# Attention and token mixing on one core: the 64-wide matmuls as four 64x64 tiles, whole-array transposes, and a written order of steps

## The chip, the core and the metric

The kernel runs on one core of one Trainium2 chip. TensorE (PE in the profile) multiplies and transposes, VectorE (DVE) and ScalarE (ACT) read its results out of PSUM, GpSimd (POOL) casts the inputs, and SyncE (SP) issues most transfers. The metric is the device time of one execution in microseconds (us); the number given for a kernel is the median over its runs.

PSUM has eight banks of 512 float32 columns on 128 partitions. A matmul names the part of the 128x128 array it uses by the partitions of its operands: 64 input partitions use half of the rows, 64 output partitions half of the columns. The profile writes this as 128\*128, 128\*64 (rows\*columns), 64\*128; a 64\*64 matmul uses one quarter.

## What is computed

```python
# q, k, v: (8 batches, 12 heads, 448 tokens, 64); float32 in and out
scores = q @ k.transpose(0, 1, 3, 2) / sqrt(64) - log(448)
attn   = sigmoid(scores)
x      = (attn @ v)  # heads side by side: (8, 448, 768)
wq, wk = x @ w_q, x @ w_k                        # (8, 448, 64) each
W_tok  = einsum('bsd,btd->bst', wq, wk) / sqrt(64)
out    = maximum(einsum('bst,btd->bsd', W_tok, x), 0) @ w_out   # (8, 448, 768)
```

The kernel works in bfloat16 with float32 sums. It never forms `W_tok`: it takes `wk` transposed times `x` first (`tmp`, 64 x 768 for a batch) and then `wq` times `tmp` (`mix`).

## The kernel before

The work is cut into 24 pairs. Pair n = (u, j) takes batches 2u, 2u+1 and heads 2j, 2j+1: four units of 448 x 448 scores. Six pairs (j = 0 to 5) make a stage u, four stages the kernel. The scheduler is off: each engine runs its instructions in the order in which the code issues them, and waits where a tile or a PSUM buffer is not ready.

For a pair, SP loads q, k (one transfer of 448 KB each) and v (four transfers, since the two batches are laid out differently); POOL casts them to bfloat16. Loads run three pairs ahead for q and k (two for v), casts two ahead (one for v).

- `tr_q`, `tr_k` (L133, L148) transpose the next pair, 64 columns at a time: 14 matmuls for q, 16 for k, of which two read a tile of zeros. Two run side by side in the two column halves. DVE copies the result out.
- `scores(n, g)` (L182), g = 0 to 5: keys 128 at a time with 64 contraction rows, two matmuls side by side in the two row halves (64\*128), one per batch. The 448 keys of a head are three blocks of 128 and 64 left over; `scores_last` (L173) takes what is left over of both heads and batches with 128 rows, half of them zeros (128\*64). Each step fills one double bank and ACT takes it through one sigmoid of 896 columns (`sigmoid`, L168). Two double banks alternate.
- `values(n, h)` (L195): 128 keys of contraction, two batches side by side in the column halves, eight matmuls per head, and one DVE copy per head.
- `tr_x` (L212) transposes the result for `tmp`, again 64 at a time with zeros.
- Once a stage: `mlp_wqk` (24 matmuls), `mlp_wkn` (16 transposes), `mlp_tmp` (16), `mlp_mix` (12, each with one relu: batch 0 on DVE, batch 1 on ACT), and 14 output chunks `mlp_out` of six full matmuls (128\*128, 384 columns), a DVE copy each and two output transfers per two chunks.

The order on PE within a pair is the body of the main loop (from L359): `tr_q(n+1)`, `scores_last`, `tr_k(n+1)`, `tr_x(n-2)`, two scores, output chunks, two scores, both `values(n-1)`, two scores, and then `mlp_wqk` of the stage before (j = 0), all of `mlp_mix` (j = 1), or more chunks (j = 2 to 5). Chunks of stage u are spread over the pairs of stage u+1: four in j = 2 and 3, two in j = 4, 5, 0, 1 (four throughout in the last stage). Everything that is not a score shares four single banks. After pair 23 the tail runs the last values, the whole token mixing of stage 3 and its 14 chunks.

Of the kernel before, what the change touches and what calls it, by code (L numbers as in the profile page):

```python
# [16 lines left out]
def kernel(  # L17
# [16 lines left out]

    nc = tc.nc
    B, H, S, HD = q.shape
    D = H * HD
# [19 lines left out]
    p_w32 = pool("w32", 3)  # L57
# [6 lines left out]
    p_o = pool("o", 4)  # L64
    ps_s = pool("ps_s", 2, space=bass.MemoryType.PSUM)
    ps_f = pool("ps_f", 4, space=bass.MemoryType.PSUM)

    NV = 3
    v32 = [singles.tile([P, 2, 2, 4, HD], F32, name=f"v32{n}") for n in range(NV)]
# [7 lines left out]
    zero16 = singles.tile([P, NP], BF16)  # L77
# [7 lines left out]
    ld = {}  # L85

    def load1(n, nm, eng):
# [10 lines left out]
    def load_v(n, eng):  # L98

        u, j = pairs[n]  # L100
        t = v32[n % NV]
        for b2 in range(2):
            base = v[2 * u + b2, 2 * j]
            for par in range(2):
                s0, s1, i0 = ((0, 4, 0), (0, 3, 4), (1, 4, 0), (0, 4, 3))[2 * b2 + par]
                eng.dma_start(
                    out=t[HALF[par], b2, :, s0:s1, :].rearrange("p h s d -> p h (s d)"),
                    in_=bass.AP(
                        base.tensor, base.offset + i0 * HD,
                        [[NI * HD, NP], [S * HD, 2], [1, (s1 - s0) * HD]],  # L110
                    ),
                )

    def cast1(n, nm, eng):
        t16 = p_c16.tile([P, 2, NI, HD], BF16, tag=nm + "16", name=nm + "16")
        eng.tensor_copy(  # L116
            out=t16.rearrange("p b i d -> p b (i d)"), in_=ld.pop((nm, n))
        )
        ld[nm + "16", n] = t16

    v16s = {}

    def cast_v(n):
        t = p_v16.tile([P, 2, 2, 4, HD], BF16, tag="v16", name="v16")
        nc.gpsimd.tensor_copy(  # L125
            out=t.rearrange("p b h s d -> p (b h s d)"),
            in_=v32[n % NV].rearrange("p b h s d -> p (b h s d)"),
        )
        v16s[n] = t


    qts, kts = {}, {}

    def tr_q(n):
        ps = ps_f.tile([P, NI, 2, NP], BF16, tag="f", name="ptq")
        t16 = ld.pop(("q16", n))
        for i in range(NI):
            for b2 in range(2):
                nc.tensor.transpose(  # L139
                    ps[HALF[b2], i].rearrange("p h n -> p (h n)"), t16[:, b2, i, :], ident16  # L140
                )
        t = p_qk.tile([P, 2, S], BF16, tag="qt", name="qt")
        nc.vector.tensor_copy(  # L143
            out=t.rearrange("p h (i n) -> p h i n", i=NI), in_=ps.rearrange("p i h n -> p h i n")
        )
        qts[n] = t

    def tr_k(n):  # L148
        ps = ps_f.tile([P, 8, 2, NP], BF16, tag="f", name="ptk")
        t16 = ld.pop(("k16", n))  # L150
        order = (0, 4, 1, 5, 2, 6, 3, 3)
        for pos in range(8):
            for b2 in range(2):
                src = zero16 if (pos, b2) in ((6, 1), (7, 0)) else t16[:, b2, order[pos], :]
                nc.tensor.transpose(  # L155
                    ps[HALF[b2], pos].rearrange("p h n -> p (h n)"), src, ident16
                )
        t = p_qk.tile([P, 2, 4 * P], BF16, tag="kt", name="kt")
        nc.vector.tensor_copy(  # L159
            out=t.rearrange("p h (s n) -> p h s n", s=8), in_=ps.rearrange("p s h n -> p h s n")  # L160
        )
        kts[n] = t
# [4 lines left out]
    def sigmoid(n, key, sc):  # L167
        at = p_at.tile([P, 2, S], BF16, tag="at", name="at")  # L168
        nc.scalar.activation(at, sc[:, :, 0:S], ACTF.Sigmoid, bias=bias_t, scale=attn_scale)  # L169
        ats[n, key] = at  # L170

    def scores_last(n):

        sc = ps_s.tile([P, 2, 512], F32, tag="s", name="sc")
        for h in range(2):
            for b2 in range(2):
                nc.tensor.matmul(  # L177
                    sc[HALF[b2], h, 0:S], kts[n][:, h, 3 * P + 64 * b2 : 3 * P + 64 * b2 + 64],
                    qts[n][:, h, :], start=True, stop=True,
                )  # L180
        sigmoid(n, 6, sc)

    def scores(n, g):
        h, m = divmod(g, 3)
        sc = ps_s.tile([P, 2, 512], F32, tag="s", name="sc")
        for b2 in range(2):
            nc.tensor.matmul(  # L187
                sc[:, b2, 0:S], kts[n][HALF[b2], h, m * P : (m + 1) * P], qts[n][HALF[b2], h, :],
                start=True, stop=True,
            )  # L190
        sigmoid(n, g, sc)


    xts = {}

    def values(n, h):
        u, j = pairs[n]
        ps = ps_f.tile([P, S], F32, tag="f", name="pv")
        for m in range(4):
            for b2 in range(2):  # L200
                slot = m + b2 if m < 3 else 3 * (1 - b2)
                rhs = ats[n, 3 * h + m][:, b2, :] if m < 3 else ats[n, 6][:, h, :]
                nc.tensor.matmul(  # L203
                    ps[HALF[b2]], v16s[n][:, b2, h, slot, :], rhs, start=(m == 0), stop=(m == 3)
                )
        t = p_x.tile([P, S], BF16, tag=f"xt{2 * j + h}", name="xt")
        nc.vector.tensor_copy(out=t, in_=ps)  # L207
        xts[u, 2 * j + h] = t
# [4 lines left out]
    def tr_x(n):  # L213
# [3 lines left out]
        ps = ps_f.tile([P, 4, 2, 2, HD], BF16, tag="f", name="px")  # L217
        for h in range(2):
            for m in range(4):
                for par in range(2):  # L220
                    i = 2 * m + par
                    src = xts[u, 2 * j + h][:, i * NP : (i + 1) * NP] if i < NI else zero16
                    nc.tensor.transpose(ps[HALF[par], m, :, h, :], src, ident16)  # L223
        nc.vector.tensor_copy(  # L224
            out=xns[u][:, :, :, 2 * HD * j : 2 * HD * (j + 1)].rearrange("p m b x -> p (m b) x"),
            in_=ps.rearrange("p m b h d -> p (m b) (h d)"),
        )


    wqk, wkn, tmps, mxs = {}, {}, {}, {}  # L230

    def mlp_wqk(u):
        ps = [ps_f.tile([P, S], F32, tag="f", name="pw") for _ in range(2)]
        for h in range(H):
            for b2 in range(2):
                nc.tensor.matmul(  # L236
                    ps[b2], wqk16[HALF[b2], h, :], xts[u, h][HALF[b2]],
                    start=(h == 0), stop=(h == H - 1),
                )
        wqk[u] = [p_one.tile([P, S], BF16, tag=f"wqk{b2}", name="wqk") for b2 in range(2)]  # L240
        for b2 in range(2):
            nc.vector.tensor_copy(out=wqk[u][b2], in_=ps[b2])

    def mlp_wkn(u):
        ps = ps_f.tile([P, 4, 2, P], BF16, tag="f", name="pk")
        for b2 in range(2):
            for m in range(4):
                for par in range(2):
                    i = 2 * m + par
                    src = wqk[u][b2][:, i * NP : (i + 1) * NP] if i < NI else zero16  # L250
                    nc.tensor.transpose(ps[HALF[par], m, b2, :], src, ident16)  # L251
# [3 lines left out]
        )  # L255

    def mlp_tmp(u):
        tmps[u] = p_one.tile([P, D], BF16, tag="tmp", name="tmp")
        for nb in range(2):
            ps = ps_f.tile([P, NB], F32, tag="f", name="pt")  # L260
            for m in range(4):
                for b2 in range(2):
                    nc.tensor.matmul(  # L263
                        ps[HALF[b2]], wkn[u][:, m, 64 * b2 : 64 * b2 + 64],
                        xns[u][:, m, b2, nb * NB : (nb + 1) * NB],
                        start=(m == 0), stop=(m == 3),
                    )
            nc.vector.tensor_copy(out=tmps[u][:, nb * NB : (nb + 1) * NB], in_=ps)  # L268

    def mlp_mix(u, c):  # L270
        if c == 0:
            mxs[u] = [p_one.tile([P, 2, S], BF16, tag=f"mx{n}", name="mx") for n in range(NC)]
        ps = [ps_f.tile([P, S], F32, tag="f", name="pm") for _ in range(2)]
        for b2 in range(2):
            nc.tensor.matmul(  # L275
                ps[b2], tmps[u][HALF[b2], c * P : (c + 1) * P], wqk[u][b2][HALF[b2]],
                start=True, stop=True,
            )
        nc.vector.tensor_scalar(mxs[u][c][:, 0, :], ps[0], moe_scale, 0.0, ALU.mult, ALU.max)  # L279
# [173 lines left out]
```

## Time and profile before

| | us |
|---|---|
| median of 3 runs (250.43 to 252.59) | 250.77 |
| the profiled execution | 250.65 |
| its span, first to last instruction | 248.5 |
| a stage in mid-kernel, from values to values (112.19 to 167.07) | 54.9 |
| from the last scores (216.86) to the end | 31.6 |

The profiled execution spends 2.15 us outside its span. A row of the grouped view reads: line, engine, operation, result from sources, shape, count, then busy time, the mean duration of one in ns, and the idle time before it. Durations on PE overlap: a matmul of 448 columns lasts about 0.36 us from issue to its modelled end, while in a dense stream a pair of them side by side passes in about half of that. So the PE durations that count here are taken from the chain of waits, where each piece ends where the next begins.

### The profile page before, as it was taken

The numbers are of one execution on the slowest core, as the hardware profiler recorded it, in microseconds if no ns is written. First come the engines' busy times: TensorE is split into PE (matmuls) and PEld (weight loads), VectorE is DVE, ScalarE is ACT, GpSimd is POOL, SyncE is SP. The second block draws the span as 40 slices with busy tenths as digits, with TensorE's granted clock in tenths as the row PEclk, the third lists the DMA queues.
The fourth block names the chain that finished last, engine by engine and source line by source line (L and its number), as shares of the span: only waits on it lengthen the run. The fifth ranks groups of instructions, "written<-read, shape, count | busy, mean of one in ns | idle before, by whom it ended". The sixth has DMA issues, their size and how long they took to land.

```text
span 248.5 us, 6124 instructions
## 1 busy us (share of the span) xinstructions
PE 215.9 (87%) x2480; PEld 116.7 (47%) x2480; DVE 132.2 (53%) x230; ACT 171.7 (69%) x194; POOL 75.5 (30%) x84
## 2 busy tenths in 40 slices
PE   0878777779779999999979999999979999998992
PEld 0534334445435644545544554455444554453660
DVE  2423444454575555564685654655684564458551
ACT  2499889986677768986688678895698678724000
POOL 1655466566302131441633041343631010000000
PEclk9979999999979999999999999999999999999997
DMA  6999999999900498789872489789962543220376
GB/s 239 303 286 268 249 330 318 308 296 262 247 2 21 115 275 231 187 231 286 224 216 65 114 240 263 211 234 259 234 170 66 130 105 95 67 63 3 79 201 163
DMA packets 35387, 47.58 MB, mean 191 GB/s; under 512 B 6432, under 2 KB 31008, under 8 KB 35360
## 3 DMA queue, kind: packets, MB, share of 16 engines
q1 hardware_dynamic: 35088, 46.74, 70.2%
q8 instruction: 19, 0.31, 0.6%
q10 hardware_dynamic: 272, 0.46, 0.5%
q14 instruction: 8, 0.07, 0.1%
HBM read 36.18 MB, written 11.01 MB: 190 GB/s over the span
## 4 chain that ended last, share of the span: by engine, by line
PE 72%; ACT 17%; issue 5%; DVE 2%; DMA 2%; ACTq 0%
PE po L289 19%; PE pv L203 16%; ACT at L169 15%; PE sc L187 12%; PE ptk L155 5%; PE ptq L139 5%; PE sc L177 5%; PE px L223 4%; PE pw L236 4%; ACT mx L280 2%; PE pt L263 2%; DMA q<-in_q_dram 2%; PE pm L275 1%; DVE tmp L268 1%; PE pk L251 1%
## 5 line engine op out<-in xcount | busy, mean ns | idle before, releaser
L169 ACT ACTIVATE at<-sc,bias_t 128x896 bf16<-128x896 f32 x168 | 158.8, 1006 | 49.3 <-PE sc L177 23.7
L289 PE MATMUL po<-wout,mx 128*128 128x384 bf16 x336 | 59.6, 327 | 0.1
L187 PE MATMUL sc<-qt,kt 64*128 64x448 bf16 x288 | 47.2, 358 | 14.4 <-ACT at L169 14.0
L294 DVE COPY o<-po 128x384 f32<-128x384 f32 x56 | 31.2, 558 | 37.7 <-PE po L289 36.6
L207 DVE CAST xt<-pv 128x448 bf16<-128x448 f32 x48 | 30.0, 625 | 39.6 <-PE pv L203 36.4
L289 PEld LDWEIGHTS <-mx 128*128 128x128 bf16 x336 | 30.6, 98 | 25.2 <-issue 7.2
L203 PE MATMUL pv<-at,v 128*64 128x448 bf16 x384 | 40.9, 356 | 0.0
L116 POOL CAST q<-q 128x896 bf16<-128x896 f32 x23 | 21.5, 933 | 59.0 <-DMA q<-in_q_dram 29.9
L125 POOL CAST v<-v 128x1024 bf16<-128x1024 f32 x24 | 25.0, 1040 | 38.4 <-PE pv L203 21.0
L187 PEld LDWEIGHTS <-kt 64*128 64x128 bf16 x288 | 12.3, 93 | 43.3 <-issue 40.8
L116 POOL CAST k<-k 128x896 bf16<-128x896 f32 x24 | 22.6, 940 | 24.5 <-DMA k<-in_k_dram 16.9
L203 PEld LDWEIGHTS <-v 128*64 128x64 bf16 x384 | 19.7, 109 | 17.0 <-issue 6.1
L159 DVE COPY kt<-ptk 128x1024 bf16<-128x1024 bf16 x24 | 16.6, 690 | 9.7 <-PE ptk L155 9.7
L139 PE MATMUL ptq<-ident,q 128*64 128x128 bf16 x336 | 15.5, 238 | 6.0 <-DVE q L116 6.0
L143 DVE COPY qt<-ptq 128x896 bf16<-128x896 bf16 x24 | 15.0, 624 | 8.6 <-PE ptq L139 8.5
L139 PEld LDWEIGHTS <-q 128*64 128x64 bf16 x336 | 11.3, 119 | 14.2 <-issue 6.5
L280 ACT ACTIVATE mx<-pm 128x448 bf16<-128x448 f32 x24 | 11.7, 550 | 8.1 <-PE pm L275 8.0
L155 PEld LDWEIGHTS <-k 128*64 128x64 bf16 x336 | 15.1, 120 | 4.2 <-issue 0.8
L224 DVE COPY xn<-px 128x1024 bf16<-128x1024 bf16 x24 | 16.4, 681 | 0.4 <-PE px L223 0.4
L177 PE MATMUL sc<-qt,kt 128*64 128x448 bf16 x96 | 14.5, 382 | 2.2 <-ACT at L169 2.2
L155 PE MATMUL ptk<-ident,k 128*64 128x128 bf16 x336 | 16.4, 233 | 0.0
L279 DVE TENSOR_SCALAR mx<-pm 128x448 bf16<-128x448 f32 x24 | 13.8, 619 | 2.6 <-PE pm L275 2.4
(36 smaller groups left out, 125.5 us busy)
## 6 DMA issues: line engine op xcount, KB each, us to landing
q<-in_q_dram SPq DMA_DIRECT2D x24, 448.0 KB, 5.9
out_dram<-o SPq DMA_DIRECT2D x56, 192.0 KB, 2.7
k<-in_k_dram SPq DMA_DIRECT2D x23, 448.0 KB, 7.0
v<-in_v_dram SPq DMA_DIRECT2D x48, 128.0 KB, 6.0
v<-in_v_dram SPq DMA_DIRECT2D x48, 96.0 KB, 5.6
w<-in_moe_w_out_dram SPq DMA_DIRECT2D x6, 384.0 KB, 6.2
k<-in_k_dram ACTq DMA_DIRECT2D x1, 448.0 KB, 4.9
wqk<-in_moe_w_q_dram SPq DMA_DIRECT2D x2, 192.0 KB, 6.4
```

The source lines that it names most:

```text
L116: eng.tensor_copy(out=t16.rearrange("p b i d -> p b (i d)"), in_=ld.pop((nm, n)))
L125: nc.gpsimd.tensor_copy(out=t.rearrange("p b h s d -> p (b h s d)"), in_=v32[n % NV].rearrange("p b h s d -> p (b h s d)"),)
L139: nc.tensor.transpose(ps[HALF[b2], i].rearrange("p h n -> p (h n)"), t16[:, b2, i, :], ident16)
L155: nc.tensor.transpose(ps[HALF[b2], pos].rearrange("p h n -> p (h n)"), src, ident16)
L169: nc.scalar.activation(at, sc[:, :, 0:S], ACTF.Sigmoid, bias=bias_t, scale=attn_scale)
L177: nc.tensor.matmul(sc[HALF[b2], h, 0:S], kts[n][:, h, 3 * P + 64 * b2 : 3 * P + 64 * b2 + 64], qts[n][:, h, :], start=True, stop=True,)
L187: nc.tensor.matmul(sc[:, b2, 0:S], kts[n][HALF[b2], h, m * P : (m + 1) * P], qts[n][HALF[b2], h, :], start=True, stop=True,)
L203: nc.tensor.matmul(ps[HALF[b2]], v16s[n][:, b2, h, slot, :], rhs, start=(m == 0), stop=(m == 3))
L207: nc.vector.tensor_copy(out=t, in_=ps)
L280: nc.scalar.activation(mxs[u][c][:, 1, :], ps[1], ACTF.Relu, bias=0.0, scale=moe_scale)
L289: nc.tensor.matmul(ps, mxs[u][c].rearrange("p b s -> p (b s)")[:, m * P : (m + 1) * P], wout16[:, c, nb * NB : (nb + 1) * NB], start=(c == ...
L294: nc.vector.tensor_copy(out=ot[0][:, nb * NB : (nb + 1) * NB], in_=ps)
```

## The change

- Scores go by 64 keys: seven steps a pair, each four matmuls of 64 rows and 64 columns, one in each quarter of the array (batch picks the rows, head the columns). `scores_last` and its zeros go. The sigmoids stay 168 of 896 columns.
- Values go by 64 keys too: seven steps of four matmuls, gathered in one double bank; one DVE copy of 896 columns in place of two of 448.
- `mlp_wqk` (12 steps) and `mlp_mix` (6 steps) are cut from two 64\*128 matmuls to four 64\*64 a step.
- All transposes take 128 x 128: seven for q, seven for k, eight for x, eight for `mlp_wkn`. The zero tile goes; `xt` and `wqk` get 64 zero columns at the end, written once by POOL (seven memsets).
- v is loaded and cast as q and k are: one transfer in place of four.
- PSUM: three double banks in turn (scores, values, wqk, mix) and two single ones.
- The order on PE is a string for each pair, with one letter a step: S scores, P values of pair n-1, q and k transposes for n+1, x `tr_x(n-2)`, W wqk, N wkn, U tmp, M mix, O a chunk. Chunks now start in j = 2 (four, then three a pair), 13 in a stage; three are left for the tail.
- At the start 44 small matmuls on the identity run before the first transposes, k of pair 0 is cast half by POOL and half by ACT, and the first copies are split by head. In the tail ACT shares the copies and issues half of the output transfers. `o` has three buffers (four before), `w32` two (three), `mx` two (one).

Core of the diff:

```diff
-    ps_s = pool("ps_s", 2, space=bass.MemoryType.PSUM)
-    ps_f = pool("ps_f", 4, space=bass.MemoryType.PSUM)
+    free2 = ["a", "b", "c"]
+    free1 = ["d", "e"]
...
-            in_=dict(q=q, k=k)[nm][2 * u : 2 * u + 2, 2 * j : 2 * j + 2].rearrange(
+            in_=SRC[nm][2 * u : 2 * u + 2, 2 * j : 2 * j + 2].rearrange(
...
+        for i in range(NI):
+            nc.tensor.transpose(
+                ps[:, i].rearrange("p h n -> p (h n)"),
+                t16[:, i].rearrange("p b d -> p (b d)"), ident16,
+            )
...
+    def scores(n, i):
+        fb, sc = bank2("sc")
+        for b2 in range(2):
+            for h in range(2):
+                nc.tensor.matmul(
+                    sc[HALF[h], b2, 0:S], qk["k", n][HALF[b2], h, i, :],
+                    qk["q", n][HALF[b2], h].rearrange("p i n -> p (i n)"), start=True, stop=True,
+                )
+        at = p_at.tile([P, 2, S], BF16, tag="at", name="at")
+        nc.scalar.activation(at, sc[:, :, 0:S], ACTF.Sigmoid, bias=bias_t, scale=attn_scale)
+        free2.append(fb)
...
+        for h in range(2):
+            for b2 in range(2):
+                nc.tensor.matmul(
+                    ps[HALF[b2], h, 0:S], ld["v16", n][HALF[h], i, b2, :],
+                    ats[n, i][HALF[h], b2, :], start=(i == 0), stop=(i == NI - 1),
+                )
+        if i == NI - 1:
+            nc.vector.tensor_copy(out=xts[j][:, :, 0:S], in_=ps[:, :, 0:S])
+            free2.append(fb)
...
+        ("SqkSPPPSxSSPPPPSS",) * 6,
...
+            "S qk S PPP S x S O S PPPP S O S O",
...
-    mlp_wqk(NU - 1)
+    run(N, "xPPPPPPP WWWWWWWWWW OO WW")
```

The first string is that of stage 0, the second that of j = 3, 4 and 5 of the later stages. The string of j = 0 holds seven S, seven P, qk, x and twelve W; that of j = 1 seven S, N, qk, x, seven P, two U and four M; that of j = 2 adds the last two M and four O.

ACT's queue around the mixing of stage 0 (`at` a sigmoid, `mx` a relu of 448 columns). Before:

```order
L90 DMA k_106<-in_k_dram 128x2x448
L328 ACT_TABLE_LOAD
L328 ACTIVATE warm<-bias_t 128x1
L169 ACTIVATE at<-sc,bias_t 128x896 x56
L280 ACTIVATE mx<-pm 128x448 x6
L169 ACTIVATE at<-sc,bias_t 128x896 x42
```

And now:

```order
L354 CAST k_180<-k_112 128x7x64
L158 ACTIVATE at<-sc,bias_t 128x896 x55
L257 ACTIVATE mx<-pm 128x448 x2
L158 ACTIVATE at<-sc,bias_t 128x896
L257 ACTIVATE mx<-pm 128x448 x2
```

The six relus stood in one block after the last sigmoid of j = 1; they now come in twos between its last sigmoids and the first of j = 2.

DVE's queue from the mixing of stage 0 through j = 2 of stage 1 (`xn` copies of `tr_x`, `xt` of values, `o` of chunks). Before:

```order
L279 TENSOR_SCALAR mx<-pm 128x448 x6
L143 COPY qt<-ptq 128x896
L159 COPY kt<-ptk 128x1024
L224 COPY xn<-px 128x8x128
L294 COPY o<-po 128x384 x2
L207 CAST xt<-pv 128x448 x2
```

And now:

```order
L259 TENSOR_SCALAR mx<-pm 128x448 x2
L195 COPY xn<-px 128x4x128 x2
L299 COPY o<-po 128x384
L177 CAST xt_102<-pv 128x2x448
L299 COPY o<-po 128x384 x3
L137 COPY qt<-ptq 128x896
L137 COPY kt<-ptk 128x896
```

The chunk copies are spread singly over the pair instead of in two twos; values take one copy a pair, and `tr_x` two.

More of the change, by code (lines that the diff above doesn't have):

```diff
@@ L148, in tr_k @@
[L148 to L162, printed above, removed]
@@ L216, in tr_x @@
             xns[u] = p_x.tile([P, 4, 2, D], BF16, tag="xn", name="xn")
-        ps = ps_f.tile([P, 4, 2, 2, HD], BF16, tag="f", name="px")
+        fb, ps = bank([P, 4, 2, 2, HD], BF16, "px")
         for h in range(2):
             for m in range(4):
[L220 to L235, printed above, removed]
+                nc.tensor.transpose(
+                    ps[:, m, h].rearrange("p b d -> p (b d)"), xts[j][:, h, m * P : (m + 1) * P],
+                    ident16,
+                )
@@ L255, in mlp_wkn @@
         )
[L257 to L268, printed above, removed]
+        free1.append(fb)
@@ new lines, in mlp_tmp @@
+    def mlp_tmp(u, nb):
+        if nb == 0:
+            tmps[u] = p_one.tile([P, D], BF16, tag="tmp", name="tmp")
+        fb, ps = bank([P, NB], F32, "pt")
+        for m in range(4):
+            for b2 in range(2):
+                nc.tensor.matmul(
+                    ps[HALF[b2]], wkn[u][:, m, 64 * b2 : 64 * b2 + 64],
+                    xns[u][:, m, b2, nb * NB : (nb + 1) * NB],
+                    start=(m == 0), stop=(m == 3),
+                )
+        dst = tmps[u][:, nb * NB : (nb + 1) * NB]
+        if nb and u == NU - 1:
+            nc.scalar.copy(out=dst, in_=ps)
+        else:
+            nc.vector.tensor_copy(out=dst, in_=ps)
+        free1.append(fb)
@@ L282, with out_chunk @@
+        for b2 in range(2):
+            relu(mxs[u][c][:, b2, :], ps[:, b2, 0:S], b2)
+        free2.append(fb)
+    chunks = []
     ot = {}
-    def mlp_out(u, m, nb):
+    def out_chunk(tail=False):
+        u, m, nb = chunks.pop(0)
         if nb == 0:
             ot[0] = p_o.tile([P, D], F32, tag="o", name="o")
-        ps = ps_f.tile([P, NB], F32, tag="f", name="po")
+        o = ot[0]
+        fb, ps = bank([P, NB], F32, "po")
         for c in range(NC):
@@ L344 @@
-    tr_q(0)
-    tr_k(0)
+    k0 = ld.pop(("k", 0)).rearrange("p b (i d) -> p b i d", i=NI)
+    k016 = p_c16.tile([P, NI, 2, HD], BF16, tag="k16", name="k16")
+    nc.gpsimd.tensor_copy(out=k016[:, :, 0, :], in_=k0[:, 0])
+    nc.scalar.copy(out=k016[:, :, 1, :], in_=k0[:, 1])
+    ld["k16", 0] = k016
+    eq = tr(0, "q", split=True)
+    eq(slice(0, 1))
+    ek = tr(0, "k", split=True)
+    for hs in (slice(0, 1), slice(1, 2)):
+        ek(hs)
+        if hs.start == 0:
+            eq(slice(1, 2))
```

308 lines of the change are left out of this document (155 added, 153 removed), and 5 rows, old and new, of the table BASE.

## The prediction

> **What bounds the kernel now.** I read the busy shares first, then the chain of waits, then the windows between pair and pair, and last the timeline of ACT.
>
> ```profile
> PE 215.9 (87%) x2480; PEld 116.7 (47%) x2480; DVE 132.2 (53%) x230; ACT 171.7 (69%) x194; POOL 75.5 (30%) x84
> PE 72%; ACT 17%; issue 5%; DVE 2%; DMA 2%; ACTq 0%
> ```
>
> PE is the bound, but the second line shows ACT carrying a sixth of the chain: the two take turns. The windows (length, then busy us by engine) tell where. The first is stage 0 from pair 2 on, the next six the pairs j = 0 to 5 of one stage, the last the tail.
>
> ```profile
> 22.20:51.10 28.90, 22.05 (x316) 12.06 (x316) 12.76 (x21) 26.09 (x29) 17.39 (x19) 1.00 1.09 296
> 107.75:116.58 8.83, 8.54 (x110) 4.55 (x112) 4.24 (x7) 7.34 (x8) 2.10 (x3) 1.00 0.86 227
> 116.58:128.83 12.25, 10.57 (x130) 5.49 (x132) 9.16 (x17) 8.74 (x12) 5.68 (x6) 1.00 0.91 253
> 128.83:138.09 9.26, 9.26 (x105) 5.12 (x106) 5.33 (x9) 7.31 (x9) 2.85 (x3) 1.00 0.20 51
> 138.09:147.34 9.25, 9.25 (x105) 5.07 (x106) 5.35 (x9) 6.72 (x7) 1.20 (x2) 1.00 0.81 225
> 147.34:154.99 7.65, 7.37 (x93) 3.89 (x94) 4.24 (x7) 5.88 (x7) 2.34 (x3) 1.00 0.81 219
> 154.99:162.63 7.64, 7.36 (x92) 3.89 (x94) 4.24 (x7) 6.61 (x8) 3.06 (x4) 1.00 0.81 229
> 216.86:248.50 31.64, 25.48 (x212) 13.99 (x210) 17.24 (x31) 5.14 (x9) 0.00 (x0) 0.96 0.39 100
> ```
>
> In j = 2 and 3 PE never rests (9.26 of 9.26). In j = 1, the longest pair by 3 us, neither engine is full: PE 10.57, ACT 8.74 of 12.25. In stage 0 (7.2 us a pair) ACT is busy 90%. So one stage is PE-bound in four pairs and loses time to turns in two, and stage 0 is close to ACT's pace.
>
> **Prices on PE.** From the chain (start, length, piece):
>
> ```profile
> 114.31 2.27 PE pw L236 x24
> 123.10 1.32 PE pt L263 x16
> 138.09 0.51 PE ptq L139 x14
> 139.43 0.45 PE px L223 x16
> 139.88 0.63 PE sc L187 x4
> 142.57 0.48 PE sc L187 x4
> 143.05 1.64 PE pv L203 x16
> 145.28 2.06 PE po L289 x12
> 229.85 13.82 PE po L289 x84
> ```
>
> Twelve pairs of 448 columns take 2.27 us: 0.19 a group side by side. Eight pairs of transposes take 0.45: 0.056 a step. A chunk is 13.82/14 = 0.99; `tmp` 1.32. What a piece takes beyond these is the change of array shape ahead of it: twelve chunk matmuls 2.06 - 1.97 = 0.09, scores after them 0.48 - 0.38 = 0.10, values 1.64 - 1.51 = 0.13, q transposes 0.51 - 0.39 = 0.12, but scores after a column-half shape 0.63 - 0.38 = 0.25. The new shape is 64\*64, which the trace lacks, and its changes are all to or from shapes with 128 rows, nearly all of them 128\*128. The rows nearest to that are those into and out of chunks (0.09, 0.10), so I take 0.10; the ends are 0 (a change of shape gives no time back) and 0.25. A pair with chunks has ten changes now, seven before.
>
> The Trainium skill, "TensorEngine Tiling (Array Packing)", Key Properties, says that a change of tiling mode (not just of tile) drains TensorE. By that rule, the trace agrees (0.09 to 0.25 us each), it speaks against this change.
>
> **The groups of four.** Scores go from 8 pairs side by side to 7 groups, values from 8 to 7: at 0.19 that saves 0.38 us a pair. W and M keep their number of steps. Whether a group of four passes in the time of a pair is not in the trace. Its four weight loads must fit under 0.19. The nearest rows are the column-half transposes, sixteen loads of 64 columns and sixteen matmuls within 0.45, so 0.03 a load and 0.11 for four: hidden. Against it stands the length of a single load:
>
> ```profile
> L203 PEld LDWEIGHTS <-v 128*64 128x64 bf16 x384 | 19.7, 109 | 17.0 <-issue 6.1
> L289 PEld LDWEIGHTS <-mx 128*128 128x128 bf16 x336 | 30.6, 98 | 25.2 <-issue 7.2
> ```
>
> So a group lies between 0.19 and 0.19 + 0.11 = 0.30; below 0.19 it cannot go, 448 columns being streamed as before. I take 0.19. A whole-array transpose streams the same 128 columns: between 0.056 and, if its 98 ns load showed, 0.098; I take 0.056, since the chunks hide the same 98 ns load under their 0.16.
>
> **A pair in the new order.** PE: 14 groups 2.66 (14 x 0.19), 22 transposes 1.23. With j = 3 to 5: three chunks 2.97 and ten changes of shape (q-k, x and three chunks, in and out) 1.00, in all 7.86. j = 2: four chunks, two M steps 0.38, ten changes (x and one chunk adjoin): 9.23. j = 0: 12 W steps 2.28 and four changes 0.40: 6.57. j = 1: four M 0.76, N 0.45, U 1.32, eight changes 0.80: 7.22. ACT's prices:
>
> ```profile
> 10.90 5.49 ACT L169 ACTIVATE at<-sc,bias_t 128x896 bf16<-128x896 f32 x6 [0.22 <-PE sc L187]
> 22.16 6.56 ACT L169 ACTIVATE at<-sc,bias_t 128x896 bf16<-128x896 f32 x7 [0.59 <-PE sc L187]
> 126.59 2.82 ACT L280 ACTIVATE mx<-pm 128x448 bf16<-128x448 f32 x6
> 216.86 0.55 PE L187 MATMUL sc<-qt,kt 64*128 64x448 bf16 x4
> ```
>
> Six sigmoids in 5.49 us, the last one 1.01 long, are one per 0.90; a relu is 2.82/6 = 0.47. A pair is 6.3 on ACT, j = 1 6.3 + 4 x 0.47 = 8.2, j = 2 7.2. So j = 0 (6.57) is at balance, j = 1 ACT's (8.2), j = 2 to 5 PE's. Walking the strings step by step, I find no bank wait in j = 3: each S comes 0.8 to 1.4 us after the one before, and its bank (two turn while values hold the third) was freed by then. In j = 0 PE comes late three times with S (qk and WWWW 1.94, x and WWWW 1.6 apart), and ACT cannot get that time back in j = 1, where it is the bound: 1.0 lost. A stage: 6.57 + 8.2 + 9.23 + 3 x 7.86 + 1.0 = 48.6 (54.9 before). Of the 6.3 gained, j = 0 and 1 give 5.3 (21.1 to 15.8), since W and M lie between scores; the four chunk pairs give 1, the two groups saved being mostly eaten by the changes of shape.
>
> **Stage 0.** PE needs 2.66 + 1.23 + 0.40 = 4.29 a pair, ACT 6.3: sigmoids at 0.90, where values stood in one block of 1.64 before. Its cover is the loads. DMA is full there (share 1.09), and the casts wait for it:
>
> ```profile
> 0.73 0.20 POOL L329 MEMSET ident<- 128x128 f32 x1 [0.29 <-POOLq L437]
> 8.55 0.93 POOL L116 CAST k<-k 128x896 bf16<-128x896 f32 x1 [0.72 <-DMA k<-in_k_dram]
> 11.66 3.54 SPq L106 DMA_DIRECT2D v<-in_v_dram  x4
> 11.93 0.93 POOL L116 CAST q<-q 128x896 bf16<-128x896 f32 x1
> 32.36 0.93 POOL L116 CAST k<-k 128x896 bf16<-128x896 f32 x1 [0.54 <-DMA k<-in_k_dram]
> 39.43 0.93 POOL L116 CAST k<-k 128x896 bf16<-128x896 f32 x1 [1.09 <-PE sc L187]
> 46.47 0.93 POOL L116 CAST k<-k 128x896 bf16<-128x896 f32 x1 [1.44 <-PE px L223]
> ```
>
> In pair 0 the second scores stand behind the transposes of pair 1. Its k is cast by 9.48 (when it lands decides, so the warm-up matmuls and the split first copies can only help the first sigmoid), the transposes end at 10.0, the second sigmoid starts 0.5 later at 10.5 (10.90 before), and the 43rd, stage 1's first, at 10.5 + 41 x 0.90 = 47.4. k of pairs 5, 6 and 7 was cast by 33.3, 40.4 and 47.4. PE now wants it one pair earlier in the string, where pairs 4, 5 and 6 begin: at 34.8, 41.1 and, behind seven P, 49.4. That is just in time if the loads come no later than before. For them: the same bytes in the same order, v in one issue where SP spent 3.54 us on four, and longer runs. Against them: POOL's seven memsets push the cast of q of pair 2 (11.93) back by some 1.4 us (an estimate, 0.2 each as `ident`'s), still ahead of its use at about 15.5; and with two `w32` buffers SP waits for the weight casts on POOL with the next q, k and v behind it. If that or DMA makes stage 0 keep its 7.2 a pair, it costs 42.0 against the 47.4 - 10.5 = 36.9: +5.
>
> **What goes at nothing.**
>
> ```profile
> L294 DVE COPY o<-po 128x384 f32<-128x384 f32 x56 | 31.2, 558 | 37.7 <-PE po L289 36.6
> L207 DVE CAST xt<-pv 128x448 bf16<-128x448 f32 x48 | 30.0, 625 | 39.6 <-PE pv L203 36.4
> L143 DVE COPY qt<-ptq 128x896 bf16<-128x896 bf16 x24 | 15.0, 624 | 8.6 <-PE ptq L139 8.5
> L253 DVE COPY wkn<-pk 128x512 bf16<-128x512 bf16 x4 | 1.7, 416 | 0.0
> out_dram<-o SPq DMA_DIRECT2D x56, 192.0 KB, 2.7
> ```
>
> DVE has in a chunk pair q and k at 0.62, `xt` at 2 x 0.625 at most, `xn` at two of 512 columns like `wkn` (0.83), three `o` at 0.56: 5.0 us under PE's 7.86. If a copy came late, PE would stand before the next of the two single banks, with the scores behind it and ACT behind those; but a bank comes round after 1.4 us or more, twice the longest copy. An `o` tile is filled each 5 us and its transfer lands in 2.7, so three buffers do.
>
> **Tail.**
>
> ```profile
> 217.33 1.91 ACT L169 ACTIVATE at<-sc,bias_t 128x896 bf16<-128x896 f32 x2 [0.45 <-PE sc L187]
> 226.63 3.12 PE L275 MATMUL pm<-wqk,tmp 64*128 64x448 bf16 x12
> 243.70 0.56 DVE L294 COPY o<-po 128x384 f32<-128x384 f32 x1 [0.42 <-PE po L289]
> ```
>
> From the last scores: themselves 0.19, O 1.09, x 0.45, P 1.43, ten W 1.90, two O 2.08, two W 0.48, copy and N 1.35, O 1.09, U 1.42, M to the first chunk 3.2 (226.63 to 229.85, kept: two engines share the same relus), 14 chunks 13.82, and 4.0 for the last copy and transfer (243.70 to 248.5 is 4.8; the copy is halved and the transfers stand in two queues, an estimate between 3.5 and 4.8): 32.5, where it was 31.6. Three chunks more lie in it, and fill waits of about 2 us.
>
> **Sum.** 47.4 + 3 x 48.6 = 193.2 for where a next sigmoid would start; the last scores begin 1.9 earlier (216.86 to 217.33, so 0.47 from scores to sigmoid, and 0.19 + 1.19 for themselves and the O behind them): 191.3. With the tail 223.8, with the 2.15 outside the span 226.0. The profiled run (250.65) stands 0.1 under the median, which I leave out.
>
> **Rivals.**
> - *Exposed loads in groups of four (slower).* At 0.30 a group: 58 groups in j = 2 to 5 6.4, j = 0 2.0, j = 1 1.0 where PE passes ACT, so 9.4 a stage; with 2 in the tail +30: 256. It decides at +0.09 a group (24.8/30 of 0.11). For it: 109 ns a load. Against: 0.03 in the transposes. 0.08.
> - *Whole-array transposes at 0.098:* 22 x 0.042 = 0.92 a pair, in five pairs of six at most, 4.6 a stage and 1.0 in the tail: +14.8, 241. The Trainium skill, "TensorE: Matmul & The Clock Gate", Back-to-back issue gap, gives some 81 ns for a sustained matmul of 128 columns with its load; by that the sum would be 235, and no row here is of that shape. 0.10.
> - *Changes of shape at 0.25:* 44 a stage on PE's path, +6.6 each and 1.2 in the tail: 247. For it: the 0.63 row. 0.10.
> - *Changes hidden (0):* -4.4 a stage: 213. Against: every row shows 0.09 or more. 0.08.
> - *Forecast,* with stage 0 at ACT's or its old pace and half changes of these prices: 217 to 236. 0.64.
>
> **Numbers.** 226. The range 216 to 241 holds the forecast's cases, the transposes, and parts of both shape cases; outside lie the exposed loads and most of the rest, some 2 in 10. A measurement tells 1% from no change, so 248.3 and 253.3 are the bounds: slower 0.07 from the exposed loads, same 0.05 from those and the dear changes, faster 0.88.
>
> **What would show it.** Right: sigmoids back to back in stage 0 (0.90), stages of about 48.6, PE full in j = 2 to 5, four scores in about 0.3 with a change of shape. Wrong: pieces of W longer than 0.19 a step (loads), q-k pieces over 0.9 for 14 (transposes), ACT waiting for PE in stage 0 with POOL on DMA.

## The result, and the profile after

| | before | after |
|---|---|---|
| median of all runs (us) | 251.09 (250.43 to 253.03, 6 runs) | 237.74 (235.34 to 240.84, 6 runs) |
| ratio, after to before | | 0.9373, 95% interval 0.9315 to 0.943 |
| the profiled execution | 250.65 | 240.42 |
| its span | 248.5 | 238.6 |
| one stage in mid-kernel | 54.9 | 51.9 |

The change makes the kernel 6% faster. Three of its six runs, the profiled one among them, had a lower TensorE clock (in the profile 0.74 over 12.9 us in stage 1 and again in stage 3) and are left out of the ratio; the other three took 235.3 to 236.2 us. Durations are read below from stage 2, where the clock is 1.00.

First the busy shares and the chain of waits by engine, both from the page of the changed kernel:

```profile
PE 212.6 (89%) x2636; PEld 119.2 (50%) x2636; DVE 123.3 (52%) x214; ACT 176.8 (74%) x204; POOL 73.8 (31%) x91
...
PE 73%; ACT 17%; DVE 4%; issue 3%; ACTq 0%; POOL 0%; DVEq 0%; POOLq 0%
```

The shape of the bound is the old one: PE carries most of the chain, ACT a sixth. DVE has 4% where it had 2%. The windows of the changed kernel (length, then busy us by engine in the order PE, PEld, DVE, ACT, POOL, then clock, DMA share and GB/s) are stage 0 from its second sigmoid on, the pairs j = 0 to 5 of stage 2, and the tail:

```profile
10.09:46.30 36.21, 28.00 (x406) 16.10 (x399) 14.78 (x24) 36.09 (x41) 24.89 (x33) 0.95 1.04 344
100.87:108.60 7.73, 6.99 (x130) 4.09 (x122) 4.48 (x7) 6.00 (x7) 3.75 (x4) 1.00 0.89 275
108.60:118.20 9.60, 8.18 (x122) 4.64 (x118) 6.68 (x12) 8.37 (x11) 3.75 (x4) 1.00 0.70 256
118.20:128.95 10.75, 9.67 (x114) 5.06 (x110) 5.86 (x12) 8.35 (x11) 2.75 (x3) 1.00 0.15 37
128.95:136.90 7.95, 7.95 (x100) 4.19 (x96) 4.67 (x9) 6.77 (x7) 1.50 (x2) 1.00 0.89 271
136.90:144.85 7.95, 7.95 (x100) 4.19 (x96) 4.67 (x9) 6.77 (x7) 2.25 (x3) 1.00 0.74 223
144.85:152.80 7.95, 7.95 (x100) 4.22 (x100) 4.67 (x9) 6.77 (x7) 3.85 (x5) 1.00 0.90 275
205.20:238.60 33.40, 27.33 (x253) 15.33 (x252) 14.41 (x27) 8.58 (x17) 0.00 (x0) 1.00 0.47 119
```

In stage 0 ACT is busy 36.09 of 36.21: it is the bound there now. In j = 3 to 5 PE is busy 7.95 of 7.95. In j = 1 and j = 2 no engine is full: of 20.35 us together PE has 17.85, ACT 16.72, DVE 12.54. There the gain fell short.

Prices on PE, from the chain of waits of the changed kernel (start, length, piece):

```profile
129.14 0.50 PE ptq L130 x7
129.64 0.39 PE ptk L130 x7
...
131.10 0.55 PE px L190 x8
...
133.04 0.31 PE sc L153 x4
133.36 0.76 PE pv L172 x16
...
134.30 1.08 PE po L287 x6
...
208.61 1.89 PE pw L214 x40
...
220.36 12.85 PE po L287 x78
```

Ten groups of four pass in 1.89 us, four groups of values in 0.76: 0.19 a group, as the pairs did. Seven whole-array transposes take 0.39: 0.056 each. A change of shape costs 0.50 - 0.39 = 0.11 (into q), 0.55 - 0.45 = 0.10 (x), 1.08 - 12.85/13 = 0.09 (chunk) and 0.31 - 0.19 = 0.12 (scores after a chunk).

Now the mixing, where j = 1 ends and j = 2 begins. From the timeline of the changed kernel (start, length, engine, line, operation, count, and in brackets the idle time before it with its releaser):

```profile
113.42 1.01 ACT L158 ACTIVATE at<-sc,bias_t 128x896 bf16<-128x896 f32 x1 [0.51 <-PE sc L153]
...
115.16 1.01 ACT L158 ACTIVATE at<-sc,bias_t 128x896 bf16<-128x896 f32 x1 [0.73 <-PE sc L153]
...
116.22 0.38 PE L153 MATMUL sc<-qt,kt 64*64 64x448 bf16 x4 [0.79 <-ACT at L158]
...
117.98 0.38 PE L153 MATMUL sc<-qt,kt 64*64 64x448 bf16 x4 [0.51 <-ACT at L158]
...
118.90 0.62 DVE L137 COPY qt<-ptq 128x896 bf16<-128x896 bf16 x1 [0.66 <-PE ptq L130]
...
119.44 0.61 DVE L137 COPY kt<-ptk 128x896 bf16<-128x896 bf16 x1
...
119.97 1.15 DVE L259 TENSOR_SCALAR mx<-pm 128x448 bf16<-128x448 f32 x2
120.62 1.07 ACT L257 ACTIVATE mx<-pm 128x448 bf16<-128x448 f32 x2 [0.91 <-DVE mx L259]
121.22 0.76 PE L172 MATMUL pv<-at,v 64*64 64x448 bf16 x12 [1.07 <-ACT mx L257]
```

Three things happen in a row. ACT idles 0.51 and 0.73, because a block of seven values and then both halves of `tmp` stand ahead of the next scores on PE. Then PE idles 0.79 and 0.51, because ACT works off sigmoids and relus in turn and the three double banks are all full. Last, DVE takes its two relus only at 119.97: the copies of q and k stand ahead of them in its queue. ACT's half of the same tile follows DVE's, so ACT waits 0.91, and the values on PE wait 1.07 for the bank.

### The profile page after: what moved, and what is told of

It reads as the page before. It is cut to its first block, busy times and chain, and to the rows that moved or that the text cites. A ratio compares the mean times of both kernels' runs of the same rounds, so it can differ in the third digit from the quotient of the medians.

```text
span 238.6 us, 6369 instructions
## 1 busy us (share of the span) xinstructions
PE 212.6 (89%) x2636; PEld 119.2 (50%) x2636; DVE 123.3 (52%) x214; ACT 176.8 (74%) x204; POOL 73.8 (31%) x91
## 2 busy tenths in 40 slices
DMA packets 28252, 47.59 MB, mean 199 GB/s; under 512 B 5312, under 2 KB 24000, under 8 KB 28224
## 4 chain that ended last, share of the span: by engine, by line
PE 73%; ACT 17%; DVE 4%; issue 3%; ACTq 0%; POOL 0%; DVEq 0%; POOLq 0%
PE po L287 25%; PE sc L153 15%; ACT at L158 14%; PE pv L172 12%; PE ptq L130 5%; PE px L190 5%; PE pw L214 4%; PE ptk L130 3%; PE pt L243 2%; PE pwarm L344 2%; ACT mx L257 2%; DVE mx L259 1%; DVE kt L137 1%; DVE xt L177 1%; PE pk L230 1%
## 5 line engine op out<-in xcount | busy, mean ns | idle before, releaser
L153 PE MATMUL sc<-qt,kt 64*64 64x448 bf16 x672 | 64.6, 372 | 15.6 <-ACT at L158 14.0
L153 PEld LDWEIGHTS <-kt 64*64 64x64 bf16 x672 | 22.6, 106 | 48.4 <-issue 38.9
L172 PE MATMUL pv<-at,v 64*64 64x448 bf16 x672 | 40.9, 359 | 2.3 <-ACT mx L257 2.3
L177 DVE CAST xt<-pv 128x896 bf16<-128x896 f32 x24 | 26.2, 1092 | 22.7 <-PE pv L172 22.7
L117 POOL CAST v<-v 128x896 bf16<-128x896 f32 x24 | 22.5, 937 | 32.9 <-PE pv L172 17.3
L195 DVE COPY xn<-px 128x512 bf16<-128x512 bf16 x48 | 18.1, 419 | 22.5 <-PE px L190 22.5
L172 PEld LDWEIGHTS <-v 64*64 64x64 bf16 x672 | 20.9, 109 | 12.7 <-issue 4.4
L137 DVE COPY qt<-ptq 128x896 bf16<-128x896 bf16 (+1 forms) x25 | 15.1, 604 | 16.6 <-PE ptq L130 16.6
L190 PE MATMUL px<-ident,xt 128*128 128x128 bf16 x192 | 15.7, 227 | 0.0
L190 PEld LDWEIGHTS <-xt 128*128 128x128 bf16 x192 | 11.7, 101 | 7.7 <-issue 7.5
L137 DVE COPY kt<-ptk 128x896 bf16<-128x896 bf16 (+1 forms) x25 | 14.9, 597 | 0.4
```

The source lines that it names most:

```text
L117: eng.tensor_copy(out=t16.rearrange("p i b d -> p b i d"), in_=ld.pop((nm, n)).rearrange("p b (i d) -> p b i d", i=NI),)
L137: nc.vector.tensor_copy(out=t[:, hs], in_=ps[:, :, hs, :].rearrange("p i h n -> p h i n"))
L153: nc.tensor.matmul(sc[HALF[h], b2, 0:S], qk["k", n][HALF[b2], h, i, :], qk["q", n][HALF[b2], h].rearrange("p i n -> p (i n)"), start=True, ...
L172: nc.tensor.matmul(ps[HALF[b2], h, 0:S], ld["v16", n][HALF[h], i, b2, :], ats[n, i][HALF[h], b2, :], start=(i == 0), stop=(i == NI - 1),)
L177: nc.vector.tensor_copy(out=xts[j][:, :, 0:S], in_=ps[:, :, 0:S])
L190: nc.tensor.transpose(ps[:, m, h].rearrange("p b d -> p (b d)"), xts[j][:, h, m * P : (m + 1) * P], ident16,)
```

## The experiments

All times are us; the ratio, formed as above, is to the kernel before, run beside each. "Stage" goes from the q transposes of one j = 0 to those of the next; "mixing" from the transposes of wk (N, in j = 1) to the q transposes of j = 3. Both are read at clock 1.00, in stage 2 or in the stage named; blank where no such stretch is whole or the marks don't fit the order. For e5, the new tiles in the old order, the stage goes from W to W.

| kernel | median (range) | ratio, 95% interval | stage | mixing |
|---|---|---|---|---|
| the changed kernel | 237.74 (235.34 to 240.84) | 0.9373 (0.9315 to 0.943) | 51.93 | 20.34 |
| e1_relu_one_engine | 235.94 (235.43 to 236.71) | 0.9401 (0.9352 to 0.9451) | 51.76 | 20.17 |
| e2_j1_spread | 239.24 (238.11 to 241.25) | 0.9515 (0.9457 to 0.9573) | | 20.64 (stage 3) |
| e3_both | 236.65 (235.43 to 238.06) | 0.9429 (0.937 to 0.9487) | 52.01 | 20.42 |
| e5_new_tiles_old_order | 247.30 (245.02 to 249.01) | 0.9821 (0.9748 to 0.9894) | 55.25 | |
| e6_old_tiles_new_order | 250.56 (249.82 to 251.22) | 0.9969 (0.9941 to 0.9998) | 54.84 | |
| e7_chunks_in_waits | 233.98 (233.88 to 234.47) | 0.9302 (0.925 to 0.9355) | 51.93 | |
| e8_mix_before_qk | 232.73 (232.54 to 235.28) | 0.9277 (0.9212 to 0.9342) | 50.97 | 19.38 |
| e9_chunks_and_mix | 232.71 (232.13 to 233.44) | 0.9255 (0.9207 to 0.9302) | 50.69 | |
| e10_mix_first_and_spread | 235.34 (233.18 to 236.09) | 0.9347 (0.9274 to 0.9421) | 51.22 | 19.62 |
| e11_mix_single_banks | 244.74 (243.41 to 245.58) | 0.9718 (0.9637 to 0.9798) | | |
| e12_mix_first_one_engine | 233.44 (232.92 to 233.91) | 0.9285 (0.9226 to 0.9345) | 50.83 | 19.24 |
| e13_values_inside_mix | 239.93 (239.18 to 241.76) | 0.9564 (0.9502 to 0.9626) | 52.43 (stage 1) | 20.83 (stage 1) |

### Two suspects apart and together: the shared relu and the blocks in j = 1

The relus of one mix tile were given to one engine, in turns:

```diff
-        for b2 in range(2):
-            relu(mxs[u][c][:, b2, :], ps[:, b2, 0:S], b2)
+        relu(mxs[u][c], ps[:, :, 0:S], c % 2)
```

> Each mix step is read out by one engine alone, DVE and ACT in turn, 896 columns at once, instead of half by each. Theory (serial readout): in the changed kernel ACT's relu waits for DVE's of the same double bank, so a bank is held 0.62 + 0.55 us; with one engine a step, two steps are read beside each other, and PE's wait of 1.07 us ahead of the values in j = 2, ACT's gap of 0.91 us there and part of PE's 0.79 and 0.51 go: 1.0 to 1.5 us a stage, 3 to 4.5 in all, 231 to 233 us. Rival (three double banks are too few for scores and mix in turn, whoever reads them): no change, 235 to 236.5. Rival (ACT is simply full there): no change either, with ACT at 100% in the mixing.

The values and the halves of `tmp` were spread between the scores of j = 1:

```diff
-            "S N S qk S x S PPPP PPP S U U S MM S MM",
+            "S N PP S qk S x PP S PPP U S U S MM S MM",
```

> The string of j = 1 is spread: N with two P, x with two P, three P with one U, one U, instead of seven P in a row and both U in a row. Theory (ACT starves twice in j = 1, for 0.51 and 0.73 us, behind 1.5 us of PE work without a score): 0.8 us a stage, 2.5 in all, 233 us. Rival (a stage is PE's, an idle ACT costs nothing): no gain, or 0.2 us a stage lost to two more changes of shape, 235.5 to 236.5.

And both edits in one kernel:

> Both edits together. Theory (two separate losses): the gains add, 228.5 to 231. Rival (both are the same idle time of a chain through the mixing): no better than the better of the two alone.

None of the three shortens the mixing by more than 0.2 us. (The second's time, 239.24, comes with mean clocks of 0.963 to 0.986 in its runs, so the mixing is what can be compared.) That two engines read one tile one after the other, which the timeline shows, costs some 0.2 a stage at most here; and a wait taken from ACT in j = 1 comes back elsewhere (below, with e10).

### Tiles and order apart

The new tiles, banks, start and tail, with the order of the kernel before written as strings:

```diff
-        ("SqkSPPPSxSSPPPPSS",) * 6,
+        ("qSkxSSSSPPPPPPPSS",) * 6,
...
-            "S N S qk S x S PPPP PPP S U U S MM S MM",
+            "qSkxNSSOSSPPPPPPPUUSSMMMMMM",
...
-            "S qk S PPP S x S O S PPPP S O S O",
+            "qSkxSSOOSSPPPPPPPSSOO",
```

> The changed kernel with its new tiles, start and tail, but the steps of a pair in the old order: all seven P in one block, two chunks together, W and M in a block, chunks as 4, 4, 2, 2, 1, 1 a pair. Theory (order and tiles both count): stage 0 back to about 7.0 us a pair (+4), j = 0 and 1 back to 8.4 and 11.9 (+3 a stage), the chunk pairs 8.5 with four and 7.1 with two chunks (-1 a stage): 244 to 247. Rival (the tiles give the gain, the order nothing): 235 to 238. Rival (the order gives all of it): 250.

And the tiles, banks, start and tail of before in the new order (L is its scores of what is left over, V a head's values):

```diff
-        scores_last(n)
...
-            values(n - 1, 0)
-            values(n - 1, 1)
...
+        ("LqkSVSxSSVSS",) * 6,
...
+            "L qk S V S x S O S V S O S O",
```

> The kernel before with its own tiles, transposes, loads, start and tail, but with the steps of a pair in the new order (values a head at a time, wqk by heads, tmp by halves, mix in twos, single chunks; scores_last in the place of the first S; mx in two buffers). Theory (the 64x64 tiles are what makes the fine order cheap, since scores, values, wqk and mix then share one shape): stage 0 falls to 6.3 to 6.5 us a pair (-5), but a chunk pair has 13 changes of shape, many of them into 64*128 at 0.25 us, and takes 9.1; a stage stays near 55, the tail gets three chunks (+3): 247 to 251. Rival (the order gives the gain whatever the tiles): stages near 52, 239 to 241.

One mid-kernel stage in windows (columns as above): of the kernel before (from values to values), the changed one, and then old tiles in the new order, with a pair of its stage 0 ahead:

```profile
112.19:167.07 54.88, 52.34 (x622) 28.00 (x624) 32.55 (x55) 42.60 (x49) 17.38 (x18) 1.00 0.74 204
```

```profile
102.77:154.70 51.93, 48.69 (x644) 26.39 (x644) 31.03 (x54) 43.02 (x49) 17.00 (x19) 1.00 0.66 210
```

```profile
30.97:37.71 6.74, 5.64 (x82) 3.05 (x78) 3.16 (x5) 6.51 (x8) 4.04 (x5) 1.00 1.07 320
108.72:163.56 54.84, 53.41 (x617) 27.27 (x618) 32.20 (x55) 43.72 (x48) 17.43 (x18) 1.00 0.73 198
```

Old tiles leave PE 53.4 us of work in a stage, so the finer order has little to close: 54.84 against 54.88, with a chunk less in it. It gains in stage 0 only (6.74 a pair, 7.2 before), and its three more chunks in the tail use that up. New tiles in the old order have less work on PE (busy 50.3 of the stage's 55.25), but the blocks keep PE and ACT taking turns (6.47 a pair in stage 0). So 251.0 goes to 250.6 by the order alone, to about 247 by the new tiles with their banks, loads, start and tail, and to about 236 by both: most of the gain is in the pair of them. Neither single figure is clean. The old block of six mix steps now shares three double banks with the scores, where before it had four single banks beside the scores' own; and in the old tiles values still go a head at a time. Banks, loads, start and tail were not tried apart from the tiles.

### Filling the waits, and taking DVE's away

Four chunks of a stage were carried into the next, one into j = 0 and three into the mixing of j = 1; j = 2, 4 and 5 do one less each. So stage 1, which has none to take over, does ten, stages 2 and 3 do fourteen, and four are left for the tail (three in the changed kernel):

```diff
-            "S PPPP S PPP S qk WWWW S x WWWW S WW S WW S",
-            "S N S qk S x S PPPP PPP S U U S MM S MM",
-            "S qk MM S PPP S x O S PPPP S O S O S O",
+            "S PPPP S PPP S qk WWWW S x WWWW S WW O S WW S",
+            "S N O S qk S x S PPPP PPP S U U S MM O S MM O",
+            "S qk MM S PPP S x O S PPPP S O S O S",
...
-            "S qk S PPP S x S O S PPPP S O S O",
+            "S qk S PPP S x S O S PPPP S S O",
```

> Four chunks of each stage are carried into the next stage, one into j = 0 and three into j = 1, where PE stands (0.74 us in j = 0, 1.42 in j = 1, 1.08 in j = 2). Theory (PE idles there for want of work it may do, since three double banks hold it to the pace of the readers): the chunks fill those waits; stage 1, three chunks short, -3.6 us, stages 2 and 3 with one more chunk +1.2 - 3.2 each, tail +1.0: -6.6, 229 us. Rival (the mixing is a chain of steps that a chunk only makes longer): stages 2 and 3 +1.2 each, 235 us.

The stage is as long as the changed kernel's, with fourteen chunks in place of thirteen: what four chunks found in waits is about a chunk's worth, 1.1 us a stage, far from all of the miss. The time, 233.98, is nearer the rival's 235 than the theory's 229.

Only the place of two mix steps against the q and k transposes was changed:

```diff
-            "S qk MM S PPP S x O S PPPP S O S O S O",
+            "S MM qk S PPP S x O S PPPP S O S O S O",
```

> In j = 2 the last two mix steps stand ahead of the q and k transposes, so that DVE takes their relus ahead of the two copies of q and k. Theory (DVE's order: the relu waits 1.1 us behind those copies, the bank behind the relu, and the values behind the bank): the 1.07 us wait ahead of the values goes, PE waits some 0.4 for the mix banks instead, 0.6 a stage, 234 us. Rival (PE waits as long for the mix banks): no change.

From its timeline, the relus, copies and values that answer to the last rows of the one above; each line is from the view of one engine:

```profile
115.85 0.98 ACT L257 ACTIVATE mx<-pm 128x448 bf16<-128x448 f32 x2
```

```profile
115.10 1.16 DVE L259 TENSOR_SCALAR mx<-pm 128x448 bf16<-128x448 f32 x2 [0.61 <-PE pm L267]
116.17 0.61 DVE L137 COPY qt<-ptq 128x896 bf16<-128x896 bf16 x1
```

```profile
116.53 0.74 PE L172 MATMUL pv<-at,v 64*64 64x448 bf16 x12
```

DVE's relus start at 115.10, ahead of the copies, ACT follows with no idle time, and the values stand there without a wait. The stage is 0.96 shorter, the mixing too. So this wait was DVE's queue, and it cost 1.0 a stage.

Both edits together:

> The edits of the two runs before together. Theory: 227.5 to 228.5. Rival (both close the same wait): as the better of the two.

Its median is that of the better of the two, as the rival had it. But the stage says otherwise: it does fourteen chunks in 50.69, where the mix ahead of q and k alone does thirteen in 50.97. In its mixing a chunk stands where PE waited 0.79 and 0.51 for ACT in the changed kernel, and the scores behind the chunks wait for nothing (PE's view, stage 2):

```profile
113.33 1.15 PE L287 MATMUL po<-wout,mx 128*128 128x384 bf16 x6
114.41 0.38 PE L153 MATMUL sc<-qt,kt 64*64 64x448 bf16 x4
...
115.38 1.15 PE L287 MATMUL po<-wout,mx 128*128 128x384 bf16 x6
116.46 0.38 PE L153 MATMUL sc<-qt,kt 64*64 64x448 bf16 x4
```

So at clock 1.00 the two edits add up. The times don't show it. The clock may be why: its four runs have mean clocks of 0.978 to 0.985, three of the four with the mix alone 0.990 to 0.998, and from 63 to 70 us its profile has 0.76 where the other has 1.00. These two kernels are the fastest of all, 232.7: both beat before and the changed kernel, and which of the two is faster at the same clock stays open.

### What is left of the miss: four more trials

The mix ahead of q and k, with the spread j = 1 of the second experiment:

> The last two mix steps ahead of q and k in j = 2, as in e8, and j = 1 spread as in e2. Theory (in e2 the time that ACT won in j = 1 was lost again at the bank held behind DVE's copies; with that gone the 0.5 and 0.7 us that ACT stands behind seven P and two U are worth something): 0.5 to 0.8 us a stage under e8's 232.7, 230.5 to 231. Rival (PE is the bound of the stage there, ACT's gaps cost nothing): 232.5 to 233.5.

ACT's queue in j = 1 of stage 2:

```profile
107.73 1.01 ACT L158 ACTIVATE at<-sc,bias_t 128x896 bf16<-128x896 f32 x1 [0.19 <-PE sc L153]
109.04 1.01 ACT L158 ACTIVATE at<-sc,bias_t 128x896 bf16<-128x896 f32 x1 [0.30 <-PE sc L153]
110.69 2.09 ACT L158 ACTIVATE at<-sc,bias_t 128x896 bf16<-128x896 f32 x2 [0.65 <-PE sc L153]
```

ACT's idle time is 1.14 in three pieces in place of 1.24 in two (0.51 and 0.73 without the spread, as in the changed kernel). Until the mixing PE has the same work to do (transposes, values, `tmp`), and however it is dealt out, ACT is done with it no sooner. The stage is 51.22, 0.25 longer than without the spread, so the theory fails.

The mix on the two single banks, one step between two scores, so that it leaves the ring of three alone:

```diff
-        fb, ps = bank2("pm")
+            fbs, pss = zip(*[bank([P, S], F32, "pm") for _ in range(2)])
...
+            "S N x S PP S U S U S PP M S PPP M S qk",
+            "S M S PPP M S qk S PPPP M S x M S O S O O",
```

> Mix steps of the first three stages go through the two single banks, so that DVE's and ACT's relus have a bank each and the three double banks are left to scores and values; N and x come first in j = 1, U and M are spread one to a score through j = 1 and 2, and a chunk moves from j = 2 to j = 3. Theory (the ring of three double banks, each held until its reader is done, couples PE and ACT in the mixing): a stage near the sum of PE's steps, 48.5 to 49.5, that is 228 to 230.5. Rival (with DVE's order mended as in e8 nothing is left but PE's own work and latencies): 232 to 234.

Its median is 9 us above the changed kernel's three faster runs, and 12 above that with the mix ahead of q and k on the ring. Some 5 us of this is a lower clock, by an estimate: in its profile the clock is 0.76, 0.79 and 0.86 for 7, 8 and 12 us in the three mixings, and length times what is missing to 1.00 gives 1.7 each. The rest is in waits. Pieces of its chain of waits in the mixing of stage 1, ahead of the lower clock:

```profile
62.00 0.62 DVE mx L259
...
62.67 0.56 PE ptq L130 x7
...
63.80 0.62 DVE kt L137
...
64.47 0.41 PE sc L153 x4
```

Transposes now wait for a single bank until DVE has taken a relu out of it, and scores until DVE has copied k: DVE stands in PE's path. So this trial moved the wait to the two single banks, which the transposes need too; what the ring alone costs it does not tell.

The mix ahead of q and k with the one-engine relu of the first experiment:

> e8 with each mix step read out by one engine, as in e1. Theory (serial readout of one bank by two engines costs, and was hidden in e1 by the wait that e8 removed): 0.3 to 0.7 us a stage under e8, 230.5 to 232. Rival (serial readout costs nothing, DVE's order was all): 232.5 to 233.

No difference beyond the intervals (a stage of 50.83 against 50.97). And the values of j = 1 set between the mix steps:

```diff
-            "S N S qk S x S PPPP PPP S U U S MM S MM",
-            "S MM qk S PPP S x O S PPPP S O S O S O",
+            "S N x S U S U S qk S MM PPPP S PPP MM S",
+            "MM S qk S PPP x S O S PPPP S O S O S O",
```

> e8_mix_before_qk with the seven values steps of j = 1 moved from ahead of the second transposed product (tmp) to between the second and third mix tile, and the last two mix tiles behind the last score of j = 1. The work is the same. In e8_mix_before_qk PE waits about 3 us a stage for ACT around the mixing (from 111.33 to 115.12 in stage 2), and ACT idles about 1.2 us earlier, behind the block of values (1.32) and behind tmp (1.42). Theory (the rest of the miss is a matter of phases: ACT has its relus in one lump that three banks cannot smooth, so PE's work must lie inside the lump): values fill PE's wait and ACT has its scores earlier, a stage of 50.97 goes to 49.6 to 50.2, the time to 228.5 to 230.5. Rival (with one of the three banks held by values, only two are left for scores and mix tiles, and the wait only changes its place, as in the other orders): a stage of 50.8 or more, 232 to 236.

Its timeline, stage 2, ACT's view and then DVE's:

```profile
105.89 6.04 ACT L158 ACTIVATE at<-sc,bias_t 128x896 bf16<-128x896 f32 x6
...
116.58 1.08 ACT L257 ACTIVATE mx<-pm 128x448 bf16<-128x448 f32 x2 [0.88 <-DVE mx L259]
```

```profile
114.93 1.09 DVE L177 CAST xt<-pv 128x896 bf16<-128x896 f32 x1 [1.38 <-PE pv L172]
115.94 1.14 DVE L259 TENSOR_SCALAR mx<-pm 128x448 bf16<-128x448 f32 x2
```

ACT's early idle time is gone, six sigmoids back to back, as the theory wanted. But now the copy of the values stands ahead of two relus on DVE, ACT waits 0.88 for those, and the mixing, read in stage 1, is 20.83 long (19.38). Three stages 1.46 longer are 4.4 of the 7 us lost. Both expected times were missed; it is the slow side of the rival, by the mechanism that the mix ahead of q and k had removed.

## Why the prediction came out as it did

The range (216 to 241) and the sign held; the value, 226.0, was 11.7 too low, 9.3 to 10.2 against the runs without the lower clock. That the range held is in part luck: its upper end, 241, was set by dear transposes, which did not come, and none of its cases was a longer mixing. Step by step:

- **A group of four at 0.19:** right. The load of a 64x64 tile lasts as long as the prediction feared, and is hidden all the same (grouped view of the changed kernel):

```profile
L153 PEld LDWEIGHTS <-kt 64*64 64x64 bf16 x672 | 22.6, 106 | 48.4 <-issue 38.9
```

- **Whole-array transposes at 0.056, changes of shape at 0.10:** right, 0.056 and 0.09 to 0.12. The rivals of 0.098, of 0.25 and of no price fell. So did the 81 ns that the Trainium skill, "TensorE: Matmul & The Clock Gate", Back-to-back issue gap, gives for a sustained matmul of 128 columns: here it is 56, in runs of seven and eight. The Trainium skill, "TensorEngine Tiling (Array Packing)", Key Properties, says that a change of mode drains TensorE; the trace shows only the time of a change, and 0.09 to 0.12 us agrees with it.
- **Chunk pairs 7.86:** 7.95, PE never idle. **j = 0, 6.57 and 1.0 for late scores:** 7.73.
- **Stage 0 at ACT's pace:** right. ACT's view of the changed kernel:

```profile
10.09 39.94 ACT L158 ACTIVATE at<-sc,bias_t 128x896 bf16<-128x896 f32 x44 [0.20 <-PE sc L153]
```

  44 sigmoids follow each other without a gap, 0.90 apart, from 10.09 (forecast 10.5). The cover of that step, loads and casts, held.
- **"j = 1 ACT's (8.2), j = 2 to 5 PE's"** with j = 2 at 9.23: this step failed. The two pairs took 9.60 and 10.75: 20.35 where the sum has 17.43. With 0.2 in j = 0 and 0.3 in the chunk pairs a stage was 3.3 longer than the 48.6 forecast, 10 in three stages, and that is the gap; the longer tail (0.8), the earlier start (0.4) and 1.8 us outside the span in place of 2.15 about cancel. I took the larger of PE and ACT over a whole pair, as if the banks could carry work from one end of it to the other.
- **DVE "at nothing":** wrong at one place. It was argued from a chunk pair, where it holds. In j = 2 the q and k copies stand ahead of the relus in DVE's queue; that cost 1.0 of the 3.3, shown by moving two mix steps.
- **The other 2.3 a stage.** The chain of the kernel with the mix ahead of q and k shows three stretches from N on: PE without a pause for 6.3 us, until 111.33; ACT for 3.8 us, with sigmoids and relus in turn; PE again, from 115.12:

```profile
105.05 0.55 PE pk L230 x8
...
111.41 1.01 ACT at L158
...
114.18 0.89 ACT mx L257 x2
...
115.12 0.38 PE pm L267 x4
```

  Each engine is the bound in its own stretch and waits in the other's. That PE could have done other work in ACT's stretch is shown: with both edits, the chunks and the mix ahead of q and k, its waits there close, and a stage does one chunk more (1.1) in 0.28 less, which is 1.4 of the 2.3. The last 0.9 is not removed by any run. That three banks, which hold no more than three tiles, are what ties the two engines together is argued: it fits all rows, but the other trials only moved the wait (to ACT, to a single bank, to DVE), and no run had more banks. What the mixing could reach stays open.
- **Tail 32.5:** 33.3 from the last scores at 205.32. Its chain, at the turn from W to N:

```profile
212.59 0.56 DVE o L299
213.15 0.60 DVE wqk L220
...
213.77 0.54 ACT wqk L221
...
214.36 0.40 PE pk L230 x4
```

  "Two W" and "copy and N" were put at 0.48 and 1.35, and from the end of the two O to the end of N it takes 2.2: a chunk's copy stands ahead on DVE, and the halves of `wqk` go one after the other. The end after the last chunk, put at 4.0, takes 4.4 (234.2 to 238.6): the halves of the last copy, too, go one after the other.

## What to carry to other kernels

When two engines are close, take the larger of the two not over a loop body but over a stretch as long as the buffers between them can carry (here three tiles, by the reading above), and add the stretches up. Where one engine must wait for the other, put work there that needs only itself: a chunk more a stage passed in such waits. Walk the queue of each engine that "costs nothing" at the places where work of two kinds meets: a 1.2 us pair of copies ahead of a relu cost 1.0 us a stage on an engine that was half idle. A smaller price per step and a finer order may each be worth little and be worth a lot together, so neither should be judged by a trial of the one without the other.

## What was not expected of the hardware

- Four matmuls of 448 columns on four quarters of the array, with four loads of 106 to 109 ns each, pass at 0.19 us a group over ten groups: the loads were hidden although each lasts more than half of a group.
- The changed kernel moved its 47.6 MB in 28,252 packets (35,387 before), and stage 0 ran at 344 GB/s with a DMA share of 1.04 (before, from pair 2 on, 296 at 1.09). The packets go with the new tiles and loads and not with the order: new tiles in the old order have 28,252 too, old tiles in the new order 35,387. That it is v's one transfer was not tried apart.
